# Moving the softmax denominators ahead of the O products in a recurrent attention forward

## The chip, the cores and the metric

The kernel runs on one NeuronCore of a Trainium2 chip, in one launch. The metric is the device time of one execution in microseconds (us). The engines are named as the profile names them: PE is the matrix engine (PEld its weight loads), DVE the vector engine, ACT the scalar engine, POOL the GpSimd engine, SP the engine that issues most DMAs.

## The reference, cut to what matters

The reference is a transformer block with a memory-augmented recurrent attention and a gated feed-forward part, followed by its vector-Jacobian product; the outputs are the block's output and eleven gradients. The change touches only the attention's forward pass. That pass walks over 64 segments of 32 rows, and the first 8 rows of each segment's attention output are the memory of the next one, so the segments form a chain:

```python
for s in range(n_seg):
    h = jnp.concatenate([mem, xs], axis=1)            # 8 + 32 rows
    q, k, v = (jnp.einsum('btd,dhe->bhte', h, W) for W in (Wq, Wk, Wv))
    scores = jnp.einsum('bhqe,bhke->bhqk', q, k) * scale
    p = _softmax(jnp.where(mask, scores, -1e9), axis=-1)
    o = jnp.einsum('bhqk,bhke->bhqe', p, v)
    o = jnp.einsum('bhte,hed->btd', o, Wo)
    mem = o[:, :M, :].copy()
    outs.append(o[:, M:, :])
```

There are 32 heads of width 128 and a model width of 512.

## The kernel before

`phase2` is the attention's forward pass: a Python loop over the 64 segments, unrolled. Three heads of 40 rows each are packed into one group of 120 partitions, so 32 heads make `G` = 11 groups. The groups are worked on in `NP` = 3 parts of `PG` = 4, 4 and 3 groups; a part's result fills one PSUM bank of 128 partitions by 4 x 128 fp32.

In each segment PE runs, in this order: the K and Q projections (`proj`), the V projection's first two chunks with the transposes of K and Q between them (`v_chunk`, `turns`), the transposed scores of the three parts (`st_exp`, whose exponentials ACT writes to `ET`), the last V chunk, and then the stretch that the change touches:

- `den(pi, ps)`: the softmax denominators of part `pi`. For each group one product of the group's 128 x 128 block of `ET` with a column of ones; the result is one column of the fourth quarter of the PSUM tile `or2` (columns 0 to 3 for part 0, 4 to 7 for part 1, 8 to 10 for part 2).
- `pv(pi)`: the O product of part `pi`, for each group `ET` times `Vst`. Parts 0 and 1 have banks of their own (`or0`, `or1`); part 2 goes to the first three quarters of `or2`, the bank that also holds all denominators.
- `recip(a, b, ps)`: DVE writes the reciprocals of parts `a` to `b-1` from `or2` to `rden`.
- `ost(pi, or_ps, eng)`: the normalized O of part `pi`, `Ost`. Parts 0 and 2 are one DVE instruction each; part 1 is four instructions on ACT.
- `ott(pi)`: PE transposes `Ost`; part 0's result is copied to `OT` by DVE, parts 1 and 2 by ACT.
- `outproj()`: the output projection from `OT` and `Wo`, which starts the rest of the chain to the next segment's memory.

Between these stand fillers that depend on the segment's place in its group of four, `s4` = `s % 4`: `mask_mm` writes the additive mask of the next segment's scores into a PSUM bank (in every segment, three times); at `s4` = 3 the transposes `p1(..., 4)` of a later input tile; at `s4` = 0 (`early`) the sum `ao_b_ft` of the four segments' tail rows, with a DVE copy `ao_b_tb` behind it; at `s4` = 2 and 3 eight transposes from `fill(s4, "turn")`.

The order on each engine is the order of the program text: `self.pin(i0)` chains all of an engine's instructions of this phase. Waits between engines are put in by the framework. It takes a PSUM tile as a whole: a product that writes one part of `or2` waits for a DVE instruction that reads another part of it.

The other phases (feed-forward part, backward through the chain, weight gradients) are not touched. The functions of the listing use the line numbers of the profile.

Of the kernel before, what the change touches and what calls it, by code (L numbers as in the profile page):

```python
# [40 lines left out]
class K:  # L41
# [395 lines left out]
    def phase2(self):  # L437
# [13 lines left out]
        with ExitStack() as ctx:  # L451
# [10 lines left out]
            def ps_f32(name):  # L462
                return psp.tile([128, PG, GW], F32, name=name, tag="p")
# [31 lines left out]
            def p1(j, k=None):  # L495
                if j < NT:
                    if j not in p1s:
                        p1s[j] = p1_tile(j)
                    for i in (range(1, 5) if k is None else [k]):
                        r = p1s[j][i]()  # L500
                        if r is not None:
                            hxs[j] = r
# [52 lines left out]
            def part3(t, pi):  # L555
                return t[:, pi * PW:min((pi + 1) * PW, G * GW)].rearrange("p (g x) -> p g x", x=GW)
# [184 lines left out]
            for s in range(NS):  # L741
# [38 lines left out]
                def den(pi, ps):  # L780
                    for g in range(pi * PG, min(pi * PG + PG, G)):
                        nc.tensor.matmul(ps[:, PG - 1, g:g + 1], lhsT=ET[:, g * GW:(g + 1) * GW], rhs=self.ones[:, 0:1],
                                         start=True, stop=True)

                def recip(a, b, ps):
                    a, b = a * PG, min(b * PG, G)
                    nc.vector.reciprocal(rden[:, a:b], ps[0:120, PG - 1, a:b])
# [9 lines left out]
                def pv(pi, or_ps=None):  # L797
                    or_ps = or_ps or ps_f32("or_ps")
                    n = min(PG, G - pi * PG)
                    for j in range(n):  # L800
                        g = pi * PG + j
                        nc.tensor.matmul(or_ps[:, j, :], lhsT=ET[:, g * GW:(g + 1) * GW], rhs=Vst[:, g * GW:(g + 1) * GW],
                                         start=True, stop=True)
                    return or_ps

                def ost(pi, or_ps, eng):
                    n = min(PG, G - pi * PG)
                    if eng == "act":
                        for j in range(n):
                            g = pi * PG + j  # L810
                            nc.scalar.activation(Ost[0:120, g * GW:(g + 1) * GW], or_ps[0:120, j, :], AF.Copy,
                                                 scale=rden[:, g:g + 1])
                        return
                    nc.vector.tensor_tensor(part3(Ost, pi)[0:120, 0:n, :], or_ps[0:120, 0:n, :],
                                            rden[:, pi * PG:pi * PG + n].unsqueeze(2).to_broadcast([120, n, 128]), op=ALU.mult)
# [57 lines left out]
                    nc.sync.dma_start(VTr[:], Vst[:, :], transpose=True)  # L873
                or2 = ps_f32("or_ps")
                den(0, or2)
                or0 = pv(0)
                Pst = sb2.tile([128, G, 128], BF16, name="Pst", bufs=1)
                if s < NS - 1:
                    nc.sync.dma_start(Pst[:], ET[:, :], transpose=True)
                else:  # L880
                    nc.gpsimd.dma_start(self.w_up, io["B_w_up"].rearrange("(c p) f -> p c f", p=128))
                    nc.gpsimd.dma_start(self.w_down, io["B_w_down"].rearrange("(fc p) d -> p fc d", p=128))
                den(1, or2)
                or1 = pv(1)
                recip(0, 2, or2)
                ost(0, or0, "dve")
                ost(1, or1, "act")
                if s4 == 3:
                    p1(s // nseg_t + P1_AHEAD, 4)
                early = s4 == 0 and len(self.later) > 1  # L890
# [3 lines left out]
                if more:  # L894
                    mask_mm(more.pop(0))
                pv(2, or2)
                den(2, or2)
                recip(2, 3, or2)
                ost(2, or2, "dve")
                fill(s4, "turn")  # L900
# [1296 lines left out]
```

## Time and profile before

| | us |
|---|---|
| median of 3 runs (lowest, highest) | 3073.68 (3072.13, 3074.03) |
| the profiled execution | 3071.52 |
| its span, first to last instruction | 3069.7 |
| forward stretch, 52 to 976 us of the span | 924.0 |

The span is what the profile covers; the execution's own time lies 1.8 us above it. Mean granted TensorE clock over the span: 0.991. In the lines of the profile, "pass_ps<-Wv,hT" means that the instruction wrote the tile `pass_ps` and read `Wv` and `hT`; "x4" that four instructions are merged in the line; a bracket at the end of a line is the engine's idle time just before it and the instruction that ended the wait. A merged PE line runs from the start of its first product to the modelled end of its last; a product's own row is 0.16 us long for one column and 0.22 us for 128, and rows of successive products overlap.

### The profile page before, as it was taken

What the parts mean: (1) busy time and instruction counts of PE and PEld (TensorE: products, weight loads), DVE (VectorE), ACT (ScalarE), POOL (GpSimd) and SP (SyncE); (2) the same over time, 40 slices, a digit from 0 to 9 for tenths busy, and PEclk for the clock granted to TensorE, in tenths of its full rate; (3) what the DMA queues carried; (4) which work ended last, traced back from release to release, by engine and by line L of the source; (5) the groups of instructions that cost most, each with busy time, mean ns of one, the idle gap of its engine ahead of it and who ended that gap; (6) DMA issues with size and microseconds to landing.
All of it is one profiled execution on the core that took longest, in us unless ns stands there. A gap on an engine that the chain in (4) does not pass through costs nothing. (4 is left out here: it accounts for less than half of the span.)

```text
span 3069.7 us, 106628 instructions
## 1 busy us (share of the span) xinstructions
PE 2972.8 (97%) x44289; PEld 1859.2 (61%) x44289; DVE 1604.4 (52%) x3746; ACT 1285.6 (42%) x3179; POOL 1212.6 (40%) x2640
## 2 busy tenths in 40 slices
PE   6999999999998899989899999999999999999999
PEld 3666666666665444445567777777777754445454
DVE  5556656656655788732255555555555532322221
ACT  2555555555555433322255555555555520111011
POOL 2554555555544222211244444444444422333321
PEclk8999999999999999999999999999999999999999
DMA  9887887887887899997599999999999998666574
GB/s 303 216 220 203 219 212 208 210 217 208 213 207 253 197 229 231 226 285 242 169 246 245 245 244 247 246 248 246 244 246 252 247 280 270 205 197 220 184 243 143
DMA packets 839319, 703.53 MB, mean 229 GB/s; under 512 B 539730, under 2 KB 711794, under 8 KB 837940
## 3 DMA queue, kind: packets, MB, share of 16 engines
q1 hardware_dynamic: 713668, 486.69, 62.9%
q0 software_dynamic: 54512, 148.63, 15.5%
q10 hardware_dynamic: 70656, 61.41, 6.4%
q8 instruction: 348, 5.70, 0.8%
q14 instruction: 135, 1.11, 0.1%
HBM read 294.93 MB, written 276.35 MB: 186 GB/s over the span
## 5 line engine op out<-in xcount | busy, mean ns | idle before, releaser
L1987 PE MATMUL gps<-rows,hrows 128*128 128x512 bf16 (+2 forms) x2160 | 417.5, 355 | 0.0
L1987 PEld LDWEIGHTS <-hrows 128*128 128x128 bf16 x2160 | 211.2, 98 | 204.6
L1693 POOL COPY dOst<-RAd 96x512 bf16<-96x512 bf16 x128 | 75.1, 611 | 309.3 <-DVE RAd L63 309.3
L63 DVE CAST ot<-gps 128x512 bf16<-128x512 f32 (+3 forms) x76 | 48.1, 633 | 284.2 <-PE gps L1987 192.5
L656 PE MATMUL pass_ps<-Wv,hT 128*32 128x512 bf16 (+2 forms) x2304 | 188.2, 357 | 0.0
L61 ACT ACTIVATE ot<-gps 128x512 bf16<-128x512 f32 (+3 forms) x75 | 41.3, 551 | 350.6 <-PE gps L1987 228.0
L255 PEld LDWEIGHTS <-hT 128*32 128x32 bf16 x4096 | 125.1, 97 | 95.8 <-DMA Wq<-in_A_Wq_dram 6.2
L1991 POOL DMA_DIRECT2D out_dram<-ot x108 | 81.3, 753 | 251.0 <-DVE ot L63 134.0
L942 POOL TENSOR_TENSOR Pst<-Pst,rden 120x1408 bf16<-120x1408 bf16 x63 | 159.8, 2537 | 39.1 <-issue 23.3
L61 ACT ACTIVATE dVT<-g_ps 128x480 bf16<-128x480 f32 (+1 forms) x192 | 104.7, 545 | 97.1 <-PE g_ps L1649 96.6
L63 DVE CAST Vst<-pass_ps 96x512 bf16<-96x512 f32 x128 | 87.3, 682 | 107.4 <-ACT RBv L61 97.7
L215 PE MATMUL dh_ps<-WvT,dVT 128*32 128x512 bf16 x2048 | 133.6, 381 | 0.1
L255 PE MATMUL pass_ps<-Wq,hT 128*32 128x512 bf16 x2048 | 125.6, 383 | 6.0 <-DMA Wq<-in_A_Wq_dram 6.0
L2001 PE MATMUL gps5o<-WoT,rows 128*128 128x512 bf16 x592 | 128.3, 379 | 1.6 <-DMA rows<-OSR 1.6
L223 PE MATMUL at_ps<-Wo,OT 128*32 128x256 bf16 x4096 | 124.8, 275 | 2.6 <-DMA Wo<-in_A_Wo_dram 2.6
L656 PE MATMUL pass_ps<-Wv,hb 128*32 128x512 bf16 (+2 forms) x636 | 127.2, 345 | 0.0
L255 PE MATMUL pass_ps<-Wk,hT 128*32 128x512 bf16 x2048 | 124.3, 380 | 1.7 <-POOL hT L545 1.1
L731 POOL DMA_DIRECT2D Vst<-RBv x192 | 99.4, 523 | 64.6 <-ACT ET L778 39.9
L255 PE MATMUL pass_ps<-WoT,dyT 128*32 128x256 bf16 (+1 forms) x3072 | 122.4, 308 | 0.9 <-ACT dyT L1767 0.9
L223 PE MATMUL dhq_ps<-WqT,dQT 128*32 128x256 bf16 x4096 | 122.9, 273 | 0.0
L215 PE MATMUL dh_ps<-WkT,dKT 128*32 128x512 bf16 x2048 | 122.3, 380 | 0.0
L223 PEld LDWEIGHTS <-dQT 128*32 128x32 bf16 x4096 | 109.7, 97 | 15.7
(413 smaller groups left out, 7004.2 us busy)
## 6 DMA issues: line engine op xcount, KB each, us to landing
OSR<-Ost SPq DMA_DIRECT2D x64, 352.0 KB
OT<-OT SPq DMA_DIRECT2D x64, 352.0 KB
VT<-VTr SPq DMA_DIRECT2D x64, 352.0 KB
PS<-Pst SPq DMA_DIRECT2D x64, 352.0 KB
OT_l<-OT SPq DMA_DIRECT2D x64, 352.0 KB
Pst_l<-PS SPq DMA_DIRECT2D x64, 352.0 KB
VT_l<-VT SPq DMA_DIRECT2D x64, 352.0 KB
DVR<-rows_x POOLq DMA_DIRECT2D x64, 352.0 KB, 6.0
```

The lines of the kernel that those rows point to most:

```text
L61: return nc.scalar.activation(out, in_, AF.Copy)
L63: return nc.vector.tensor_copy(out, in_)
L215: self.nc.tensor.matmul(ps[32 * j:32 * j + 32, :], lhsT=lhsT, rhs=w, start=(n < 4), stop=(n >= total - 4), tile_position=(0, 32 * j))
L223: nc.tensor.matmul(ps[32 * j:32 * j + 32, :], lhsT=x[k], rhs=w[k][:, 256 * d:256 * d + 256], start=(n == 0), stop=(n == total - 1), tile_p ...
L255: self.nc.tensor.matmul(ps[32 * j:32 * j + 32, :], lhsT=lhs(c), rhs=rhs, start=(c == 0), stop=(c == DC - 1), tile_position=(0, 32 * j))
L656: nc.tensor.matmul(ps[32 * j:32 * j + 32, o * E:(o + n) * E], lhsT=lhsT, rhs=wc[:, 3 * a + hl:3 * (a + n - 1) + hl + 1:3, :], start=(c == ...
L731: nc.gpsimd.dma_start(Vst[96 + 8 * j:104 + 8 * j, :], rb[32 * j + o:32 * j + o + 8, :])
L942: nc.gpsimd.tensor_tensor(Pst[0:120, :, :], Pst[0:120, :, :], rden[:, :].unsqueeze(2).to_broadcast([120, G, 128]), op=ALU.mult)
L1693: nc.gpsimd.tensor_copy(dOst[0:96, 512 * hf:512 * hf + 512], RAd[0:96, 512 * hf:512 * hf + 512])
L1987: nc.tensor.matmul(ps[:, 0:ng * E], lhsT=hrows[:, tp_, c * 128:(c + 1) * 128], rhs=rows[:, tp_, 0:ng * E], start=(tp_ == 0), stop=(tp_ == ...
L1991: nc.gpsimd.dma_start(outw[c * 128:(c + 1) * 128, h0:h0 + 3 * (ng - 1) + 1:3, :], ot[:, 0:ng * E].rearrange("p (h e) -> p h e", e=E))
L2001: nc.tensor.matmul(pss[gg][:], lhsT=src[0][:, src[1], gg * E:(gg + 1) * E], rhs=dyrows[:, tp_, :], start=(tp_ == order[0]), stop=(tp_ == o ...
```

## The change

The denominators of part 1 move ahead of the first O product, and the reciprocal of parts 0 and 1 behind them (it was behind the second O product). The denominators of part 2 move from behind the third O product to in front of the fillers and the mask product that come before it. The reciprocal of part 2 keeps its place in the text. No instruction is added or removed.

```diff
                 or2 = ps_f32("or_ps")
                 den(0, or2)
+                den(1, or2)
+                recip(0, 2, or2)
                 or0 = pv(0)
                 Pst = sb2.tile([128, G, 128], BF16, name="Pst", bufs=1)
...
-                den(1, or2)
                 or1 = pv(1)
-                recip(0, 2, or2)
                 ost(0, or0, "dve")
                 ost(1, or1, "act")
+                den(2, or2)
                 if s4 == 3:
                     p1(s // nseg_t + P1_AHEAD, 4)
                 early = s4 == 0 and len(self.later) > 1
...
                 if more:
                     mask_mm(more.pop(0))
                 pv(2, or2)
-                den(2, or2)
                 recip(2, 3, or2)
                 ost(2, or2, "dve")
```

On PE the order per segment goes from den 0, pv 0, den 1, pv 1, (fillers), mask, pv 2, den 2 to den 0, den 1, pv 0, pv 1, den 2, (fillers), mask, pv 2. The order of instructions on DVE, ACT, POOL and SP is the same before and after. In the built program three waits change with it, in every segment: the first product of den 2 waits for the reciprocal of parts 0 and 1, a wait that pv 2 had; pv 2's first weight load, which waited for DVE and ACT, waits for neither; and `ost` of part 0 on DVE waits for PE (pv 0) in addition to the reciprocal. The transposing DMA of `ET` (`Pst`) stands between the same neighbours on SP.

## The prediction

> **What bounds the kernel now.** I read the page, the table by stretches, the waits of the transposes of Ost, and the timeline of single segments. Busy time by engine:
>
> ```profile
> PE 2972.8 (97%) x44289; PEld 1859.2 (61%) x44289; DVE 1604.4 (52%) x3746; ACT 1285.6 (42%) x3179; POOL 1212.6 (40%) x2640
> ```
>
> The table by stretches, for the forward pass (busy time of PE, its loads, DVE, ACT, POOL; clock, DMA share, GB/s), and the idle time ahead of L794:
>
> ```profile
> 52.00:976.00 924.00, 905.66 (x17682) 610.07 (x17682) 542.51 (x1349) 520.46 (x1442) 475.27 (x1057) 1.00 0.81 213
> ```
>
> ```profile
>   DVE Ost L814: 26.0, 96
> ```
>
> PE is busy 97% of the span and 98% of the forward stretch (905.66 of 924 us), so time goes only where PE stops or has less to do. The change removes no PE work: what it can give is a share of the stops. The last line belongs to the transposes of Ost (L794): 26 us of idle behind DVE's ost, in 48 segments (counted once for loads, once for products). The rows overlap, so a stop must exceed the overlap to be printed; the timeline shows it better. A segment with s4=1:
>
> ```profile
> 478.27 0.93 ACT L778 ACTIVATE ET<-st_ps 128x480 bf16<-128x480 f32 x2
> ...
> 478.83 0.25 PE L782 MATMUL or_ps<-ones,ET 128*128 128x1 bf16 x4
> ...
> 478.95 0.38 PE L802 MATMUL or_ps<-Vst,ET 128*128 128x128 bf16 x4
> ...
> 479.17 0.24 PE L782 MATMUL or_ps<-ones,ET 128*128 128x1 bf16 x4
> ...
> 479.27 0.38 PE L802 MATMUL or_ps<-Vst,ET 128*128 128x128 bf16 x4
> ...
> 479.49 0.37 PE L720 MATMUL st_ps<-maskT,ident 128*128 128x480 bf16 x1
> 479.51 0.21 DVE L787 RECIPROCAL rden<-or_ps 120x8 f32<-120x8 f32 x1 [0.51 <-PE or_ps L782]
> ...
> 479.76 0.69 DVE L814 TENSOR_TENSOR Ost<-or_ps,rden 120x512 bf16<-120x512 f32 x1
> ...
> 479.87 0.33 PE L802 MATMUL or_ps<-Vst,ET 128*128 128x128 bf16 x3
> 479.89 1.14 ACT L811 ACTIVATE Ost<-or_ps,rden 120x128 bf16<-120x128 f32 x4 [0.28 <-DVE rden L787]
> ...
> 480.03 0.22 PE L782 MATMUL or_ps<-ones,ET 128*128 128x1 bf16 x3
> 480.37 0.17 DVE L787 RECIPROCAL rden<-or_ps 120x3 f32<-120x3 f32 x1
> 480.50 0.38 PE L794 MATMUL tps<-ident,Ost 120*128 120x120 bf16 x4 [0.25 <-DVE Ost L814]
> 480.57 0.56 DVE L814 TENSOR_TENSOR Ost<-or_ps,rden 120x384 bf16<-120x384 f32 x1
> ...
> 480.93 0.58 PE L794 MATMUL tps<-ident,Ost 120*128 120x120 bf16 x7
> 481.04 0.40 DVE L63 COPY OT<-tps 128x480 bf16<-128x480 bf16 x1
> ...
> 481.56 0.40 PE L223 MATMUL at_ps<-Wo,OT 128*32 128x256 bf16 x8
> ```
>
> The reader is to see a chain on DVE: the second den ends at 479.41 (479.17+0.24), recip follows 0.10 later, then ost 0 (to 480.45), recip 2, ost 2 (to 481.13), the copy of OT (to 481.44), and 0.12 behind it the output projection. PE stops three times for it: before pv 2 (mask done near 479.70, pv 2 at 479.87), before the first transpose (den 2 done near 480.11, transpose at 480.50), and before the projection. The chain starts where den 1 ends, and den 1 stands behind pv 0.
>
> **The change, part by part.** *den 1 ahead of pv 0.* A den block holds PE 0.10 (479.17 to 479.27), a pv block of four 0.22 (479.27 to 479.49). den 1 starts at 478.94 instead of 479.17, so it and the reciprocal come 0.23 earlier: recip 479.28 to 479.49. pv 0 comes 0.10 later, pv 1 at its old time.
>
> The Trainium skill, "TensorE: Matmul & The Clock Gate", section "Back-to-back issue gap", gives 81 ns per product of 128 columns with its weight load. By that pv 0 would take 0.32 and the reciprocal gain 0.33; the trace's 0.055 per product decides.
>
> New waits. den 1 needs the second exponential, which ends at 478.84 (0.57 after its start at 478.27); in segment 0 den 0 followed its exponential by 0.06, so it may go at 478.90, and its slot comes at 478.93: no wait, by 0.03. In the last four segments den 0 comes 0.05 earlier: 0.02 each, nothing.
>
> *ost 0.* It now waits for pv 0 too, whose last product ends at 479.42: before the reciprocal's end. The price is a third wait. Bounds from 479.49: 0.04 as now (479.72 to 479.76), or 0.17 as for ACT's ost with four waits (479.72 to 479.89). I take 0.10, what recip itself needs from den's end with its two waits. ost 0 starts at 479.60 instead of 479.76: 0.16 earlier (bounds 0.22, held by pv 0's end plus 0.10, and 0.10). Queued behind it on DVE are recip 2, ost 2 and the OT copy, all 0.16 earlier; recip 2 finds its den done.
>
> *den 2 ahead of the fillers.* Its PE slot is 479.49, and it must wait for recip 0-1 because it writes the bank that recip reads. Queued behind it: the fillers, the mask, pv 2, the transposes. From DVE's end to a PE product: 0.05 (ost 0's end to the transpose at 480.50) to 0.15 (recip's end to pv 2, with an extra semaphore step for two waits). den 2's product has one DVE wait, so I take 0.06: den 2 at 479.55 to 479.63, mask to 479.84, pv 2 to 480.00 (before, pv 2 and den 2 ended at 480.11). The stop before pv 2 goes; 0.06 before den 2 comes.
>
> The skill's "PSUM — Partial Sum Buffer", section "PSUM bank collisions raise a hardware error", says to guard PSUM by bank, not by address; this speaks against the move, for den 2 and recip touch different columns. Were only addresses guarded, den 2 would not wait, and where PE is the late one 0.06 a segment more would be won.
>
> *ost 1 on ACT* starts 0.17 after recip (479.89), and pv 1 ends at 479.65. With recip at 479.49 pv 1 is the last; with recip's 0.10 behind PE that is 479.76, so 0.13 earlier (bounds 0 and 0.23; nearest is the former pair of rows). It ends at 480.90.
>
> *What is late next, by s4.* s4=1: transposes at 480.34, part 1's last after ACT at 480.95, part 2 at 481.03 (before 481.18), OT copied by 481.28, projection at 481.40: 0.16. s4=0: the same chain with the ao_b_tb copy in it; its sums end on PE well before ost 0 does: 0.16. s4=2: the eight "turn" transposes (0.44) hide ost 0 today; pv 2 ends 0.10 earlier, so the transposes gain 0.10, and the projection, held by DVE's OT copy, 0.16. s4=3 differs:
>
> ```profile
> 508.72 0.39 PE L418 MATMUL p1tp<-ident,h 128*128 128x128 bf16 x4
> 508.74 0.21 DVE L787 RECIPROCAL rden<-or_ps 120x8 f32<-120x8 f32 x1 [0.32 <-PE or_ps L782]
> ```
>
> Here the p1 transposes cover the reciprocal and pv 2 does not stop. den 2 in front of them does: PE loses 0.06. But the projection is held by ACT (ost 1, then the copy of p1tp, then a transpose into a freed bank), which is 0.13 earlier; PE's path then gives 0.10. Bounds: 0 (ACT does not move) to 0.14.
>
> Sum per four segments: 0.16+0.16+0.16+0.10 = 0.58; sixteen times: 9.3 us. The lower ends (0.10, 0.10, 0.09, 0) give 4.6; the upper (0.22, 0.22, 0.2, 0.14) 12.5. The rest of a segment hangs on PE's order behind the projection, so I pass the shift on whole. The projection's later weights come from ACT's copies: part 1's ends at 481.97 before and is needed near 482.05 after; cover 0.08, and with it gone the gain shrinks by what is short. SP, POOL and the DMAs keep their order. From the profiled 3071.52 this gives 3062.2; the median lies 2.2 above that execution, so 3064.4.
>
> **The rivals.** *Given back.* The shift may be eaten by something that does not move with PE: ACT's OT copies, or DMAs (busy 0.81 of the stretch). For it: that share, and the 0.08 of cover. Against it: PE waits for a DMA in this stretch only in single places of a few us in all. Time: 3073.7.
>
> *Slower: den 2 blocks PE.* One product at the head of PE's queue waits on a DVE round trip with fillers, mask and pv 2 behind it. If the release takes x after recip's end instead of 0.06, s4=2 and 3 lose it in full, since their turn transposes follow straight on, and DVE's chain helps no longer. Worked through as above, four segments together change by -0.45 at x=0.15 and by +0.32 at 0.42, so it decides from 0.3 on; at 0.51, the idle time printed ahead of recip above and the farthest row, the change is +0.68, sixteen times 10.9 us: 3084.6. For it: segment 30's timeline has recip once 0.37 late. Against it: every DVE-to-PE release at Ost shows 0.05 to 0.06.
>
> **How the numbers follow.** The forecast has 0.75, "given back" 0.16, "slower" 0.09. About 0.2%, 6.1 us, is what a measurement can tell from no change: faster is below 3067.5. Of the forecast's range (3061.2 to 3069.1) about a tenth lies above that. So faster 0.68, same 0.23, slower 0.09. The range goes from 3060.5 to 3073.5, taking in part of "given back".
>
> **What would show it.** Right: recip 0.23 earlier after den 0, the first transposes 0.16 earlier at s4=0 and 1, no stop before pv 2, a stop near 0.06 before den 2, the forward stretch 9 us shorter, all behind it unchanged. Wrong: den 1 waiting for ACT; ost 0 starting over 0.2 after recip's end; a PE stop over 0.2 before den 2; or the projection early and the next segment not.

## The result and the profile after

| | before | after |
|---|---|---|
| median us (lowest to highest, 22 runs each) | 3074.25 (3068.44 to 3080.26) | 3066.93 (3062.16 to 3073.61) |
| ratio, 95% interval | | 0.9973, 0.9967 to 0.9978 |
| first exponential of segment 1 to that of segment 63 | 902.90 | 894.13 |
| span of the profiled execution | 3069.7 | 3070.5 |

The change is faster by 0.27%, which is 8.3 us (6.8 to 10.1). All differences of whole executions in this text go by the ratio in this way; the two medians differ by 7.3 us, the means by 8.2. The forecast was 9.3 us. The profiled execution of the changed kernel shows nothing of it in its span, though its forward pass is 8.8 us shorter; where that went is looked into below (experiment 6).

The page of the changed kernel, busy time by engine; then the table by stretches for segments 1 to 63 (PE, its loads, DVE, ACT, POOL; clock, DMA share, GB/s):

```profile
PE 2970.5 (97%) x44213; PEld 1860.3 (61%) x44289; DVE 1607.4 (52%) x3746; ACT 1286.6 (42%) x3179; POOL 1213.9 (40%) x2640
```

```profile
71.92:966.05 894.13, 884.85 (x17416) 599.74 (x17413) 535.85 (x1326) 512.89 (x1420) 469.41 (x1042) 1.00 0.80 214
```

The same 17416 products are in these segments as before (the 76 product records that the page has fewer lie elsewhere); the stretch is 8.8 us shorter while PE's busy time falls by 3.5 (888.31 to 884.85, from the same view of before). The rest, 5.3 us, is PE idle time that is gone. That busy time falls at all without less work comes from overlapping rows: part of a wait lies beneath the modelled end of a product. The rows' own lengths, overlaps counted twice, add up to 5213.6 us before and 5213.2 after.

The idle time ahead of the transposes of Ost (L794), the row that the prediction started from:

```profile
  DVE Ost L814: 16.7, 67
```

It was 26.0 in 96 places. Loads and products are both counted in it; for the products alone, in segments 1 to 63, it goes from 10.0 us in 46 places to 3.3 in 18.

The timeline of the same segment as in the prediction (29, `s4` = 1), PE, DVE and ACT:

```profile
476.54 0.35 PE L782 MATMUL or_ps<-ones,ET 128*128 128x1 bf16 x8
...
476.75 0.61 PE L802 MATMUL or_ps<-Vst,ET 128*128 128x128 bf16 x8
...
477.00 0.21 DVE L787 RECIPROCAL rden<-or_ps 120x8 f32<-120x8 f32 x1 [0.29 <-PE or_ps L782]
...
477.26 0.21 PE L782 MATMUL or_ps<-ones,ET 128*128 128x1 bf16 x3
477.29 0.69 DVE L814 TENSOR_TENSOR Ost<-or_ps,rden 120x512 bf16<-120x512 f32 x1
...
477.33 0.36 PE L720 MATMUL st_ps<-maskT,ident 128*128 128x480 bf16 x1
...
477.45 1.14 ACT L811 ACTIVATE Ost<-or_ps,rden 120x128 bf16<-120x128 f32 x4
477.53 0.33 PE L802 MATMUL or_ps<-Vst,ET 128*128 128x128 bf16 x3
477.90 0.18 DVE L787 RECIPROCAL rden<-or_ps 120x3 f32<-120x3 f32 x1
...
478.05 0.38 PE L794 MATMUL tps<-ident,Ost 120*128 120x120 bf16 x4 [0.18 <-DVE Ost L814]
478.11 0.56 DVE L814 TENSOR_TENSOR Ost<-or_ps,rden 120x384 bf16<-120x384 f32 x1
...
479.10 0.51 PE L223 MATMUL at_ps<-Wo,OT 128*32 128x256 bf16 x12
```

Count from the first den (476.54 here, 478.83 before). The reciprocal starts at 0.46 instead of 0.68, ost 0 at 0.75 instead of 0.93, the first transposes at 1.51 instead of 1.67, the projection at 2.56 instead of 2.73. The eight O products hold PE until near 477.20 (0.055 each); den 2 starts at 477.26, 0.05 after the reciprocal's end at 477.21. This is the new stop. pv 2 follows the mask without one. One thing was not in the prediction: the second reciprocal starts at 477.90, when ost 0 is ending (477.98) but also just 0.04 behind the end of pv 2 (477.86). At `s4` = 3, where the p1 transposes stand before pv 2, it does wait for pv 2. Segment 31:

```profile
505.87 0.69 DVE L814 TENSOR_TENSOR Ost<-or_ps,rden 120x512 bf16<-120x512 f32 x1
...
506.33 0.33 PE L802 MATMUL or_ps<-Vst,ET 128*128 128x128 bf16 x3
...
506.69 0.18 DVE L787 RECIPROCAL rden<-or_ps 120x3 f32<-120x3 f32 x1
...
506.94 0.38 PE L794 MATMUL tps<-ident,Ost 120*128 120x120 bf16 x4
```

ost 0 ends at 506.56 and pv 2 at 506.66; the second reciprocal starts at 506.69. By the medians at `s4` = 3 it starts 1.59 after the first den, later than before (1.53). The first transposes come at 1.83 instead of 1.77, which is PE's new stop of 0.06 before den 2. The projection still starts earlier, at 2.77 instead of 2.88: before, it stood behind a transpose of PE that waited for ACT's copy of p1tp (the copy ends at 510.74, the transpose starts at 510.80 in segment 31), and ACT, whose ost 1 hangs on the first reciprocal, comes 0.15 earlier now.

The time from a segment's first exponential to the next segment's, median of the segments 4 to 59 at each `s4`, is the same to 0.01 us in two profiles of one kernel, so small shifts can be read from it. All experiments are compared in it:

| us per segment | s4=0 | 1 | 2 | 3 | sum of four | against before |
|---|---|---|---|---|---|---|
| before | 14.595 | 14.367 | 14.373 | 14.954 | 58.289 | |
| the change | 14.424 | 14.207 | 14.250 | 14.839 | 57.720 | -0.569 |
| den 1 and reciprocal alone | 14.427 | 14.200 | 14.207 | 14.802 | 57.636 | -0.653 |
| den 2 alone | 14.594 | 14.432 | 14.471 | 15.114 | 58.611 | +0.322 |
| den 2 between mask and pv 2 | 14.427 | 14.200 | 14.207 | 14.803 | 57.636 | -0.653 |
| denominators in score banks | 14.531 | 14.300 | 14.305 | 14.779 | 57.916 | -0.373 |
| change, DVE longer | 14.636 | 14.405 | 14.413 | 14.937 | 58.392 | +0.103 |
| change, PE longer | 14.427 | 14.280 | 14.325 | 14.963 | 57.995 | -0.294 |

### The profile page after: what moved, and what is told of

It reads as the page before. It is cut to its first block, busy times and chain, and to the rows that moved or that the text cites. A ratio compares the mean times of both kernels' runs of the same rounds, so it can differ in the third digit from the quotient of the medians.

```text
span 3070.5 us, 106490 instructions
## 1 busy us (share of the span) xinstructions
PE 2970.5 (97%) x44213; PEld 1860.3 (61%) x44289; DVE 1607.4 (52%) x3746; ACT 1286.6 (42%) x3179; POOL 1213.9 (40%) x2640
## 4 chain that ended last, share of the span: by engine, by line
PE 47%; issue 2%; DMA 1%; POOL 0%; SPq 0%; ACT 0%; DVE 0%; POOLq 0%
PE gps L1987 11%; PE dh_ps L215 8%; PE g_ps L1649 6%; PE pass_ps L255 5%; PE gps5o L2001 4%; PE dhq_ps L223 4%; PE dh_tps L215 3%; PE dp_ps L1626 2%; PE tps L1559 2%; PE dp_ps L1634 1%; PE turn_ps L1513 1%; PE dh_ft L323 1%; POOL out_dram L1991 0%; DMA rows<-OSR 0%; DMA rows_x<-dQT 0%
```

## The experiments

My theory was that DVE's chain from the reciprocal to the OT copy sets the projection's start, so that the gain comes from den 1 and the reciprocal, and that moving den 2 costs a little. The first rival was that the gain is the PE stop before pv 2, which the move of den 2 takes away. Baselines for the ratios are runs of the kernel before on the same chip; their medians were 3073.71 for the first four experiments and 3073.57 for the others.

### 1. One part of the change alone

Against the changed kernel:

```diff
                 ost(1, or1, "act")
-                den(2, or2)
...
                 pv(2, or2)
+                den(2, or2)
                 recip(2, 3, or2)
```

> The den of part 1 and the reciprocal of parts 0 and 1 are moved as in the change; the den of part 2 stays behind pv 2 as before. My theory (the gain is DVE's chain reciprocal, ost 0, reciprocal 2, ost 2, OT copy, which starts earlier): all of the gain stays, and the PE stop of 0.06 us before den 2 goes. Forward period of four segments 0.57 to 0.65 us shorter than before (the changed kernel has 0.57), total 9 to 10.5 us below before. Rival (the gain is the stop before pv 2, which the move of den 2 takes away): less than half of the gain is left, 0 to 4 us.

Measured: 3066.17 median of 5, ratio 0.9967 (0.9954 to 0.9979), 10.1 us below before. Per four segments -0.653, against -0.569 for the whole change. All of the gain is in this part. The 0.084 between the two is at `s4` 2 and 3, 0.043 and 0.037. (The stretch of segments 1 to 63 is only 0.2 us shorter than in the change, because in this execution segments 26 and 30 took 0.78 and 0.32 longer than in experiment 3; the medians leave such single delays out.) Segment 29:

```profile
474.83 0.37 PE L720 MATMUL st_ps<-maskT,ident 128*128 128x480 bf16 x1
...
475.04 0.33 PE L802 MATMUL or_ps<-Vst,ET 128*128 128x128 bf16 x3
```

pv 2 starts 0.21 behind the start of the mask product, where it was 0.38 before (479.49 to 479.87). So the stop before pv 2 is gone here too, though den 2 stands where it was: the earlier reciprocal takes it away, not the move of den 2. The rival falls as it was put. Whether the stop itself was the gain, this run cannot tell. Two others can: before, there is no such stop at `s4` 0 and 3 (pv 2 0.20 behind the mask in the median), and 0.171 and 0.115 are gained there all the same; and in experiment 5 the stop stays away while the gain is lost.

### 2. The other part alone

Against the kernel before:

```diff
                 ost(1, or1, "act")
+                den(2, or2)
...
                 pv(2, or2)
-                den(2, or2)
                 recip(2, 3, or2)
```

> Only the den of part 2 is moved ahead of the fillers and the mask; den 1 and the reciprocal stay where they were. My theory: den 2 then waits on PE for a reciprocal that ends 0.23 us later than in the changed kernel, about 0.29 us behind its slot, with fillers, mask and pv 2 behind it, and the second reciprocal, which reads the bank that pv 2 writes, comes later too. By s4 0, 1, 2, 3 the projection starts 0, 0.1, 0.1 and 0.25 us later: 0.45 us per four segments, total 7 us above before (range 2 to 9). Rival (moving den 2 is what helps, because the stop before pv 2 goes): 3 us or more below before.

Measured: 3079.63 median of 11, ratio 1.0017 (1.0008 to 1.0026), 5.2 us above before. The timeline of a segment with `s4` = 3 (segment 31):

```profile
507.94 0.38 PE L802 MATMUL or_ps<-Vst,ET 128*128 128x128 bf16 x4
508.19 0.21 DVE L787 RECIPROCAL rden<-or_ps 120x8 f32<-120x8 f32 x1 [0.32 <-PE or_ps L782]
...
508.45 0.21 PE L782 MATMUL or_ps<-ones,ET 128*128 128x1 bf16 x3
508.52 0.38 PE L418 MATMUL p1tp<-ident,h 128*128 128x128 bf16 x4
...
508.94 0.33 PE L802 MATMUL or_ps<-Vst,ET 128*128 128x128 bf16 x3
509.31 0.18 DVE L787 RECIPROCAL rden<-or_ps 120x3 f32<-120x3 f32 x1 [0.20 <-PE or_ps L802]
```

The four O products begin at 507.94 and hold PE until about 508.16. den 2 starts only at 508.45, 0.05 behind the reciprocal's end, and the p1 transposes, the mask and pv 2 stand behind it. The second reciprocal waits 0.20 for pv 2 (which ends at 509.27). The mechanism of the "slower" rival in the prediction is real: a den at the head of PE's queue that waits on DVE. PE stops for 0.29 here, and for 0.06 in the change, because there the reciprocal is done earlier. The parts are not additive: -0.653 and +0.322 make -0.331, and together they give -0.569. My size for this run (0.45 per four) was too large at `s4` 1 and 3 (0.065 and 0.160, expected 0.1 and 0.25).

### 3. den 2 behind the fillers

Against the changed kernel:

```diff
                 ost(1, or1, "act")
-                den(2, or2)
...
                     mask_mm(more.pop(0))
+                den(2, or2)
                 pv(2, or2)
```

> The changed kernel, but den 2 stands between the mask and pv 2, behind the fillers. My theory: the reciprocal is done before den 2's slot, so PE does not stop (0.06 us in the changed kernel); at s4 2 and 3, where PE's path is near the end of the chain, 0.03 to 0.06 us a segment are won, 0.5 to 2 us in all against the changed kernel: 9.5 to 11 us below before, and the forward period equal to the one with den 1 alone moved within 0.02 us per four segments. If the stop is hidden everywhere: the same as the changed kernel within 0.3 us of the forward stretch.

Measured: 3063.93 median of 6, ratio 0.9966 (0.9954 to 0.9978), 10.4 us below before. Each `s4` agrees to 0.001 us with experiment 1. So PE's stop of 0.06 in front of den 2 is worth 0.08 per four segments, 1.3 us in all, and nothing at `s4` = 0. This version and that of experiment 1 are the best of the study; their intervals overlap with that of the change, so that they beat it is shown by the segment times only.

### 4. The wait on the bank taken away

Against the changed kernel, the denominators go to spare columns of the score banks, whose exponentials are done; part 2 to another bank than parts 0 and 1.

```diff
-                    st_ps = masked.pop(pi)
+                    st_ps = dens[pi] = masked.pop(pi)
...
-                        nc.tensor.matmul(ps[:, PG - 1, g:g + 1], ...
+                        nc.tensor.matmul(ps[:, 0, 120 + g % 8:121 + g % 8], ...
...
-                den(0, or2)
-                den(1, or2)
-                recip(0, 2, or2)
+                den(0, dens[0])
+                den(1, dens[0])
+                recip(0, 2, dens[0])
...
-                den(2, or2)
+                den(2, dens[1])
...
-                recip(2, 3, or2)
+                recip(2, 3, dens[1])
```

> The order of the changed kernel, but the denominators go to spare columns of two score banks (parts 0 and 1 in the bank of score part 0, part 2 in that of part 1) instead of the bank of pv 2. So den 2 waits for no reciprocal, and the second reciprocal does not wait for pv 2. My theory: PE's stop before den 2 (0.06 us) is gone in every segment, and at s4 3 the second reciprocal starts up to 0.15 us earlier. s4 0 and 1 do not change (DVE's chain holds them), s4 2 gains 0.03 to 0.05, s4 3 about 0.07: 1.5 to 2 us below the changed kernel in the forward stretch, 10.5 to 11.5 below before. If the bank's waits cost nothing: the same as the changed kernel.

Measured: 3071.05 median of 11, ratio 0.9987 (0.9978 to 0.9996), 4.0 us below before: the expectation failed. Its timeline, segment 29 again (line numbers are one higher from L778 on):

```profile
476.81 0.21 DVE L788 RECIPROCAL rden<-st_ps 120x8 f32<-120x8 f32 x1 [0.32 <-ACT ET L779]
476.98 0.22 PE L783 MATMUL st_ps<-ones,ET 128*128 128x1 bf16 x3
...
477.71 0.17 DVE L788 RECIPROCAL rden<-st_ps 120x3 f32<-120x3 f32 x1
...
477.99 0.56 DVE L815 TENSOR_TENSOR Ost<-or_ps,rden 120x384 bf16<-120x384 f32 x1
```

What was aimed at came: den 2 follows the O products without a stop (its first den at 476.32, so 0.66 behind it; 0.72 in the change), and `s4` = 3 gained 0.060. But in the built program the reciprocals now wait for ACT too (which reads the same bank), and ost 2 for PE as well as for DVE. ost 2 starts 0.11 after the second reciprocal's end, where the change has 0.03 (478.08 to 478.11); the first reciprocal starts at 0.49 after the first den, against 0.46. DVE's chain is longer by such steps, 0.03 at the first reciprocal and 0.07 at ost 2 in the medians, and `s4` 0 to 2 lose 0.107, 0.093 and 0.055. That the extra waits are the reason rests on the trace of these instructions, where the steps add up to the loss at `s4` 0 and 1; it was not tried by itself.

### 5. DVE's chain and PE's work made longer

Two additions to the changed kernel, one on each engine:

```diff
                 recip(0, 2, or2)
+                nc.vector.tensor_copy(rden[:, 0:8], rden[:, 0:8])
```

> The changed kernel with one more DVE instruction behind the reciprocal of parts 0 and 1 (rden of these parts copied onto itself); PE has the same work, and den 2 does not wait for the copy. I put the copy at about 0.2 us with its wait. My theory (DVE's chain from the reciprocal on, and ACT's ost 1 that hangs on it, set the end): the projection comes 0.2 us later at s4 0 and 1, about 0.15 at s4 2 and 0.12 at s4 3, where PE has some of the lead: 0.67 us per four segments, the forward stretch 10.7 us longer than in the changed kernel, so that the total is again that of before within 3 us. Rival (the gain is PE's shorter or better filled order): no change against the changed kernel.

Measured: 3076.25 median of 11, ratio to before 1.0008 (0.9999 to 1.0017). Segments 1 to 63 take 904.87, 10.74 longer than in the change; per four segments 0.672.

```profile
538.65 0.21 DVE L787 RECIPROCAL rden<-or_ps 120x8 f32<-120x8 f32 x1 [0.29 <-PE or_ps L782]
...
538.89 0.17 DVE L878 COPY rden<-rden 120x8 f32<-120x8 f32 x1
...
539.15 0.69 DVE L814 TENSOR_TENSOR Ost<-or_ps,rden 120x512 bf16<-120x512 f32 x1
```

This is segment 33 (`s4` = 1). ost 0 starts 0.96 after the first den (538.19) instead of 0.76 in the change (medians of both runs at every `s4`), and ACT's ost 1 starts 0.14 later; pv 2 comes as in the change. The segments at `s4` 0 to 3 move by 0.212, 0.198, 0.163 and 0.098. One small DVE instruction per segment, with PE's work unchanged, takes the whole gain back: the chain on DVE, with ACT's ost 1 behind the same reciprocal, is what the change shortened.

The other addition:

```diff
                 den(2, or2)
+                den(2, or2)
```

> The changed kernel with the three products of den 2 done twice: 0.08 us more on PE per segment at the place of den 2, nothing more on DVE. My theory: hidden at s4 0 and 1, where PE waits for ost 0 anyway; up to 0.05 at s4 2, and 0.08 at s4 3, where the second reciprocal waits for pv 2: 0.13 us per four segments, 2 us in all. Rival (every 0.08 us on PE counts, since PE is busy 97 per cent): 5 us.

Measured: 3069.69 median of 11, ratio to before 0.9987 (0.9979 to 0.9996). Per four segments 0.275 more than the change, twice what I expected and nearer to the rival's 0.32: the expectation failed. `s4` 0 to 3: 0.003, 0.073, 0.075, 0.124. Segment 29:

```profile
478.31 0.29 PE L782 MATMUL or_ps<-ones,ET 128*128 128x1 bf16 x6
...
478.66 0.33 PE L802 MATMUL or_ps<-Vst,ET 128*128 128x128 bf16 x3
479.02 0.18 DVE L787 RECIPROCAL rden<-or_ps 120x3 f32<-120x3 f32 x1
```

The second reciprocal starts at 479.02, 0.03 behind pv 2's end (478.99), and 0.01 before ost 0's end (478.34 + 0.69), where in the change it overlapped ost 0 by 0.08. It waits for pv 2 because pv 2 writes the bank that it reads. So in the changed kernel two paths reach it together, ost 0 on DVE and pv 2 on PE; more of either is paid. At `s4` = 0 the ao_b_tb copy stands on DVE between ost 0 and the second reciprocal and hides pv 2: the reciprocal comes 0.04 later, ost 2 does not, and the segment pays 0.003. At `s4` = 3 more is paid than was added, because the first transpose of part 2 waits for ACT's copy of p1tp in this run (it starts 0.05 behind the copy's end), which it does not in the change.

### 6. Where the first profile lost its gain

Both kernels were profiled once more, unchanged.

> The changed kernel once more, for a second profile. In the first one the span is 0.8 us longer than before although the forward stretch is 7 to 9 us shorter; the loss lies between the end of the forward pass and the last product of the first weight gradients (line 1334). If that part merely differs from execution to execution: the forward stretch is the same to 0.3 us from segment 1 to 63, and that later part differs by some us from the first profile. If it eats the gain: the later part is again 7 us longer than in the profile of before.

> The kernel before once more, for a second profile of the same parts. If the part behind the forward pass differs from execution to execution, it differs here too by some us from the first profile of before, with the same code; segments 1 to 63 take 902.9 us again.

| us | segments 1 to 63 | end of forward to last product of L1334 | span |
|---|---|---|---|
| before, first and second profile | 902.90, 902.98 | 524.0, 527.8 | 3069.7, 3071.3 |
| the change, first and second | 894.13, 894.18 | 531.6, 528.9 | 3070.5, 3066.6 |
| den 1 alone; den 2 alone | 893.90; 907.94 | 526.1; 532.2 | 3064.4; 3080.4 |
| den 2 at pv 2 | 892.79 | 525.6 | 3060.4 |

(The end of forward is the last transpose of `Vst`; in experiment 2 the line numbers are the same.) The segments repeat to 0.1 us, while the next part differs by 3.8 and 2.6 us for the same code. It is not tied to an earlier forward end: the earliest (den 2 at pv 2) has 525.6, the latest but one (den 2 alone) 532.2, the latest (DVE longer, experiment 5) 524.2. The span of the first profile was one of the long ones. That the change itself adds nothing there is not settled to better than some 3 us by two profiles of each; the five variants of the changed kernel (experiments 1 and 3 to 5) have 524.2 to 526.3 there, and the executions, 8.3 us by the ratio against 8.8 in the segments, leave little room for it. Segment 0, which waits for the first loads, also differs: 17 to 23 us.

## Why the prediction was right, point by point

- *Bound.* That PE's stops behind DVE's chain are what can be won holds. At `s4` = 1 PE's stops up to the first transposes add up to 0.57 before (0.18 before pv 2, 0.39 before the transposes) and 0.41 after (0.06 before den 2, 0.34), by the medians; and experiment 5 gives the time back with one DVE instruction. At `s4` = 3 it is ACT's chain, behind the same reciprocal, as predicted.
- *den 1 and the reciprocal 0.23 earlier.* Measured 0.22. The exponential of part 1 was in time, as reckoned from the 0.03 of room.
- *ost 0, 0.16 earlier with 0.10 for the third wait.* It starts 0.17 earlier by the medians, and 0.09 after the reciprocal's end where it was 0.04 before, so that the wait for pv 0 cost 0.06 per segment.
- *ost 1 on ACT, 0.13 earlier.* It starts 0.15 earlier, 0.91 after the first den instead of 1.06.
- *den 2's stop of 0.06.* Measured 0.06. Experiment 3 prices it at 1.3 us; a plain move of den 1 and the reciprocal would have been better than the whole change. The prediction has the end of the stop before pv 2 under den 2's move; experiment 1 shows that the earlier reciprocal is what ends it.
- *"recip 2 finds its den done."* This step failed. It has its den, but it also waits for pv 2, since pv 2 is in front of it in the program and writes its bank. At `s4` 0 to 2 of the change pv 2 ends in time, by a hair at 1 and 2, and the wait costs nothing. At `s4` = 3 the reciprocal is held by pv 2 and starts 0.14 behind ost 0's end, where it overlapped it by 0.08 before, and ost 2 starts 0.06 later than before (1.80 after the first den). The transposes of part 2 still follow PE's other work without a stop, so the projection did not suffer; the wait showed in the total when PE's work was made longer (experiment 5, second part).
- *By s4.* Predicted 0.16, 0.16, 0.16 and 0.10; measured 0.171, 0.160, 0.123 and 0.115. `s4` = 2 was 0.04 too high: I took PE's path there as covered, but the transposes, which follow PE's own work without a stop, come only 0.11 earlier and hold the OT copy, and experiments 1 and 3 give 0.043 back when the stop goes.
- *Sum.* Predicted 0.58 per four segments, measured 0.569; over the segments 8.8 us, in the total 8.3 (6.8 to 10.1), predicted 9.3. That the sum is closer than its terms is partly luck: 0.037 too much at `s4` = 2 stands against 0.026 too little at `s4` 0 and 3.
- *The rivals.* "Given back": the projection's weights from ACT's copies did not bind (its 64 products take 1.66 us from first to last start before and after), and the projection's shift by `s4`, 0.17, 0.16, 0.13 and 0.12, arrives whole at the next segment. "Slower": the mechanism exists, as experiment 2 shows with a stop of 0.29, but in the change the reciprocal's early end leaves 0.06 of it. The row that spoke for it, the reciprocal 0.37 late in segment 30, is a single delay: both profiles of before have it in that one of segments 1 to 63, and both of the change have one of 0.34 in segment 47 instead, ahead of the OT copy. Its cause is open.

## What to carry to other kernels

When PE is 97% busy and the rest is in small stops, look for the short reductions whose results another engine turns into a scale, and issue them ahead of the large products that do not need them: four one-column products and the reciprocal behind them, moved ahead by 0.22 us, were worth 0.65 us per four segments (experiment 1), with no work saved. Do not move a product ahead of its bank's reader merely because its operands are ready: a wait at the head of an in-order queue is paid by all that stands behind it (5 us in experiment 2). A small result that shares a bank with a large product inherits that product's waits in both directions, and moving it to a bank that yet another engine reads may bring other waits that cost more (experiment 4).

## What the runs showed of the hardware that was not expected

- A DVE instruction starts later when it waits for PE as well, even where the PE product had ended before: ost 2 0.10 after its reciprocal's end (experiment 4) against 0.03 (the change, no wait for PE), though pv 2 had ended 0.30 earlier at `s4` 1 and 2; ost 0 0.09 (the change) against 0.04 (before, no wait for PE), though pv 0 had ended 0.07 earlier. These are medians; the ends of products are the modelled ones.
- Single delays on DVE stand in otherwise equal segments: the copy of experiment 5 starts 0.035 after its reciprocal in 63 segments and 0.19 in one (segment 29). One segment shown is to be held against the median of its kind.
- The 62 segments, some 900 us, repeat to 0.1 us in two profiles of each kernel, while executions of the kernel before differ as a whole by 12 us (3068.44 to 3080.26): differences of a tenth of a per cent can be read from a stage's own period when the total cannot show them.
